# Infini-attention and grouped attention on one core: B's gate moved into the reciprocal sums, and the way from head sums to weighed heads cut into stages some turns apart

## The chip, the cores and the metric

The kernel runs on one core of a Trainium2 chip. The metric is device time in microseconds (us). The core's engines are TensorE (PE, with its weight loads shown as PEld), VectorE (DVE), ScalarE (ACT), GpSimd (POOL) and SyncE (SP), which issues nearly all DMA transfers.

## The reference

Two attentions over 2048 tokens, model width 576, 32 heads of width 18, in float32; their outputs stand side by side.

```
A:  q = x @ wq (32 heads); k = x @ wk, v = x @ wv (one head, shared)
    a = softmax(q k^T / sqrt(18)) v, heads side by side, @ wo
B:  q, k, v = x @ wq, x @ wk, x @ wv (32 heads each), in 4 segments of 512
    in each segment s, for each head, with g = sigmoid(beta[head]):
      a_dot = causal softmax(q k^T / sqrt(18)) v
      a_mem = (phi(q) M) / (phi(q) z + 1e-6)        # M = z = 0 in segment 0
      o     = g * a_mem + (1 - g) * a_dot
      M += phi(k)^T v;  z += sum of phi(k)          # phi(t) = t + 1 for t > 0, else exp(t)
    o, heads side by side, @ wo
```

## The kernel before, in words

The first stage (up to about 328 us) projects x for both attentions, stores q, k and v parts in DRAM, builds B's memory M and z, and stores for segments 1 to 3 the numerators already multiplied by g (`numB`, L353 and L354) and the denominators (`denB`). At its start ACT issues small loads, among them five of `b_beta` that spread each head's beta over the 18 rows of that head (L265 to L269). From these ACT and DVE make `gt`, which is g, and `omg`, which is 1 - g (L270 to L273).

The second stage works in blocks of four heads and 512 queries: 32 blocks of A (16 tiles of 128 keys) and 32 of B (three tiles, causal). B blocks come in pairs that a fixed list (L712) places behind A blocks. Two heads' scores for a tile of keys make an item, and three items make a turn (two at a block's end). In turn k the loop at L929 emits:

1. the scores of the turn's items on PE (L765 for A, L776 for B) and their exponentials on ACT (L785). One item of three is first copied out of PSUM by DVE (L782). Some exponentials of A are worked out on DVE in nine steps (L738 to L748), two steps in a turn. B's diagonal tiles are masked by POOL (L790);
2. one step of the output projection of a finished chunk, if one is waiting (`run_fill(1)`, L662: four matmuls; a chunk has 60 such steps);
3. the products with v of the items of turn k - 2 (L815). At a block's end DVE copies the sums out (L824) and SP stores them (L826). The first of a head's 19 rows is its sum of exponentials;
4. what is due by then (`due(k)`, L948): a list of pending steps, at most two in a turn.

A chunk is one attention's 512 queries. When its block 6 is done (heads 0 to 27, tiles 0 to 3) and again when its block 7 is done (heads 28 to 31, tile 4), `finish` (L868) puts the chunk's remaining steps on that list:

- `sums` one turn later: SP loads the sums of exponentials (`sm<-oA`, `sm<-oB`), and for B's segments 1 to 3 the denominators;
- `inverses` four or five turns after that: DVE's reciprocal (L618), then stores to DRAM (`rA`, `rB`, `rdB`);
- `load_heads`, tile by tile, when there is room (L890): the heads (`o`), the reciprocals spread over each head's 18 rows (`rb`), and for segments 1 to 3 the numerators (`nb`) and their reciprocals (`rb2`). It uses four buffers for rb and three each for nb and rb2;
- `weigh` six or eight turns later, one POOL operation at a time: for B o times omg (L647), o times rb (L644), nb times rb2 (L654) and their sum (L655); for A only o times rb;
- once all five tiles are weighed, the projection of the chunk joins the queue of fill steps.

PE, ACT and DVE run in exactly the order in which the loop emits (L918). POOL and SP do not: their order comes from the scheduler, and each runs its own queue in that order, as soon as the data are there. So the turn of a step fixes its place on PE, ACT and DVE, but on POOL a mask and a weighing step stand in whatever order the scheduler gave them. A transfer on SP also waits until the eighth one before it has landed.

Of the kernel before, what the change touches and what calls it, by code (L numbers as in the profile page):

```python
# [7 lines left out]
F32 = mybir.dt.float32  # L8
# [4 lines left out]
ALU = mybir.AluOpType  # L13
# [5 lines left out]
S, D, H, DH = 2048, 576, 32, 18  # L19
NSEG, L = 4, 512  # L20
C = 512
NCH = S // C
NKT = S // 128
HT = [7, 7, 7, 7, 4]
RT = [18 * h for h in HT]
H0 = [0, 7, 14, 21, 28]
# [7 lines left out]
VW = DH + 1  # L34
# [34 lines left out]
def attention_pair_kernel(ctx, tc, a_xT, a_w, a_wo, b_xT, b_w, b_wo, b_beta, ident_d, hmask_d, bmask_d, cmask_d, sel_d, zmask_d, selx_d, sely_d, out):  # L69
    nc = tc.nc  # L70
    ctx.enter_context(nc.allow_low_precision(reason="exact splits into parts"))

    cp = ctx.enter_context(tc.tile_pool(name="cp", bufs=1))
# [13 lines left out]
    oA = [dram(f"oA{c}", [H, 32, C], F32) for c in range(NCH)]  # L87
    oB = [dram(f"oB{c}", [H, 32, C], F32) for c in range(NSEG)]
    rA = [dram(f"rA{c}", [H, C], F32) for c in range(NCH)]
    rB = [dram(f"rB{c}", [H, C], F32) for c in range(NSEG)]  # L90
    rdB = [dram(f"rdB{c}", [H, C], F32) for c in range(NSEG)]
    numB = [dram(f"numB{c}", [D, C], F32) for c in range(NSEG)]
# [4 lines left out]
    kstA = cp.tile([128, S], F32R, name="kstA")  # L97
    VA = cp.tile([128, NKT * VW + 13], F32, name="VA")
    VAv = VA[:, : NKT * VW].rearrange("p (k v) -> p k v", v=VW)
    gt = cp.tile([128, 5], F32, name="gt")  # L100
    omg = cp.tile([128, 5], F32, name="omg")
    flag = cp.tile([1, 1], I32, name="flag")
    fm = cp.tile([128, 5], F32, name="fm")
    nc.gpsimd.memset(fm, 0.0)
# [40 lines left out]
    with ExitStack() as ph:  # L145
# [75 lines left out]
        for c in range(NCH):  # L221
            if c == 0:
                xh, xl, fillx = next_x(a_xT, 0)
                for k in range(5):
                    load_wk(wAh, wAl, a_w, 0, CA, k, True)
                    fillx(k)
                nc.sync.dma_start(ident, ident_d)
            else:
                xh, xl = nx[:2]
            nx = next_x(a_xT, c + 1) if c < NCH - 1 else next_x(b_xT, 0)  # L230
            for t in (4, 0, 1, 2, 3):
                M = 114 if t == 4 else 126
                pj = ps.tile([128, C], F32, name="pj", bufs=4)
                proj(pj[:M], wAh, wAl, xh, xl, 126 * t, M)
                R = RT[t]
                if t == 4:
                    nc.vector.tensor_reduce(km[:M, c : c + 1], pj[:M], axis=AX.X, op=ALU.max, apply_absolute_value=True)
                    vT = p1.tile([128, C], F32, name="vT", bufs=2)
                    nc.scalar.copy(vT[96:114], pj[96:114])
                    pv = ps.tile([128, 4, 128], F32, name="tr", bufs=1)  # L240
                    for i in range(4):
                        nc.tensor.transpose(pv[:, i, 0:DH], vT[96:114, 128 * i : 128 * i + 128], ident[96:114, 96:114])
                    nc.vector.tensor_copy(VAv[:, 4 * c : 4 * c + 4, 1:VW], pv[:, :, 0:DH])
                nc.scalar.activation(AQ[:R, t, c * C : c * C + C], pj[:R], AF.Abs)
                R2 = 90 if t == 4 else 126
                qp = split2(pt, pj[:R2], R2)
                store_parts(qp, 0, R, qA[c], H0[t], HT[t])
                nx[2](t)

                if c == 2:  # L250
                    load_wk(wBh, wBl, b_w, 504, 648, t, False)
                if c == 3:
                    load_wk(wBh, wBl, b_w, 2 * D, D, t, False)
                if t == 4:
                    nc.sync.dma_start(kA[:, :, c * C : c * C + C], qp[72:90].bitcast(F32))
            if c == 0:
                nc.scalar.dma_start(hmask[:126], hmask_d)
                nc.scalar.dma_start(bmask[:126], bmask_d)
                nc.scalar.dma_start(sel[:114], sel_d)
                nc.scalar.dma_start(zmask[:126], zmask_d)  # L260
                nc.scalar.dma_start(selx[:126], selx_d)
                nc.scalar.dma_start(sely, sely_d)
                nc.scalar.dma_start(ones_d.rearrange("j (a b) -> (j a) b", b=128), onest)
                nc.vector.memset(gt, 0.0)
                for t in range(5):  # L265
                    lo, nh = H0[t], HT[t]
                    nc.scalar.dma_start(
                        gt[: RT[t], t : t + 1], b_beta[lo : lo + nh][:, None].to_broadcast([nh, DH])[:, :, None]
                    )  # L269
                nc.scalar.activation(gt, gt, AF.Exp, scale=-1.0)  # L270
                nc.vector.tensor_scalar(gt, gt, 1.0, None, op0=ALU.add)
                nc.vector.reciprocal(gt, gt)
                nc.vector.tensor_scalar(omg, gt, -1.0, 1.0, op0=ALU.mult, op1=ALU.add)  # L273
# [339 lines left out]
        return sm, R, w, mem  # L613

    def inverses(ab, c, lo, hi, said):
        sm, R, w, mem = said
        n = 2 if mem else 1
        nc.vector.reciprocal(sm[:R, :n], sm[:R, :n])  # L618
        r_d = rA if ab == "A" else rB
        nc.sync.dma_start(r_d[c][lo:hi].rearrange("h (s t) -> h s t", t=w), sm[:R, 0])  # L620
        if mem:
            nc.sync.dma_start(rdB[c][lo:hi].rearrange("h (s t) -> h s t", t=w), sm[:R, 1])

    def load_heads(ab, c, t):
        o_d, r_d = (oA, rA) if ab == "A" else (oB, rB)
        if (ab, c) not in parts:
            parts[ab, c] = pa.tile([128, 5, C], F32, name="o", bufs=2)
        tiles = [parts[ab, c][:, t], pa.tile([128, C], F32, name="rb", bufs=4)]
        if ab == "B" and c > 0:
            tiles += [pa.tile([128, C], F32, name=n, bufs=3) for n in ("nb", "rb2")]  # L630
        lo, n, R = H0[t], HT[t], RT[t]
        nc.sync.dma_start(tiles[0][:R], o_d[c][lo : lo + n, 1:VW, :])
        nc.sync.dma_start(tiles[1][:R], r_d[c][lo : lo + n, None, :].to_broadcast([n, DH, C]))
        if ab == "B" and c > 0:
            nc.sync.dma_start(tiles[2][:R], numB[c][DH * lo : DH * lo + R])
            nc.sync.dma_start(tiles[3][:R], rdB[c][lo : lo + n, None, :].to_broadcast([n, DH, C]))
        return tiles

    def weigh(ab, c, t, tiles):

        R = RT[t]
        o, rb = (x[:R] for x in tiles[:2])
        v = nc.gpsimd
        own = lambda: v.tensor_tensor(o, o, rb, op=ALU.mult)  # L644
        if ab == "A":
            return [own]
        part = lambda: v.tensor_scalar(o, o, omg[:R, t : t + 1], None, op0=ALU.mult)  # L647
        if len(tiles) == 2:
            return [part, own]
        nb, rb2 = (x[:R] for x in tiles[2:])  # L650
        return [
            part,
            own,
            lambda: v.tensor_tensor(nb, nb, rb2, op=ALU.mult),  # L654
            lambda: v.tensor_tensor(o, o, nb, op=ALU.add),  # L655
        ]

    def out_part(ab, c, i, t, dst, c0, n, start, stop):

# [193 lines left out]
    def at(k, cost, ready, step):  # L853
        later.append((k, cost, ready, step))
        later.sort(key=lambda e: e[0])
# [12 lines left out]
    def finish(k, ab, c, hg):  # L868

        ts = range(4) if hg == 6 else range(4, 5)  # L870
        lo, hi = (0, 28) if hg == 6 else (28, 32)
        box = {}
        weighed.setdefault((ab, c), 0)
        last = (ab, c) == blocks[-1][:2]
        d1, d2 = (2, 3) if last else (4, 6) if (ab, c) == ("B", 0) else (5, 8)

        def begin(k):
            summing.add(hg)
            box[0] = sums(ab, c, lo, hi)
            at(k + d1, 0, lambda: True, inv)  # L880

        def inv(k):
            inverses(ab, c, lo, hi, box[0])
            summing.remove(hg)
            for t in ts:
                at(k, 0, room, lambda k, t=t: load(k, t))

        def room():

            return loaded[0] < (3 if ab == "B" and c > 0 else 4) and ((ab, c) in parts or len(parts) - filled[0] // FILL < 2)  # L890

        def load(k, t):
            loaded[0] += 1
            box[t, t] = load_heads(ab, c, t)
            at(k + d2, 1, lambda: True, lambda k, t=t: heads(k, t))

        def heads(k, t):
            if not isinstance(box[t, t][0], type(heads)):
                box[t, t] = weigh(ab, c, t, box[t, t])
            box[t, t].pop(0)()  # L900
            if box[t, t]:
                at(k, 1, lambda: True, lambda k: heads(k, t))
                return
            loaded[0] -= 1
            weighed[ab, c] += 1
            if weighed[ab, c] == 5 and not last:
                at(k + 1, 0, lambda: True, lambda k: fill.append(out_proj(ab, c)))

        at(k + (0 if last else 1), 0, lambda: hg not in summing, begin)

    def split(n, cut):

# [127 lines left out]
```

## Time and profile before

| | us |
|---|---|
| three timed runs | 1466.11, 1469.55, 1471.54 (median 1469.55) |
| the profiled execution | 1471.9 |
| its span, first to last instruction | 1470.2 |
| output projection, L662 (3680 matmul records) | from 486 us on, one step a turn |
| L790 masks on POOL | 94.2 (192) |
| L644 o times rb on POOL | 54.5 (40) |
| L647 o times omg on POOL | 32.6 (20) |
| L654, L655 on POOL | 21.4, 21.5 (15 each) |
| L745 on DVE, one of the exponential's steps | 142.4 (192), mean 0.741 |

Read the profile by turns: in the timeline of PE, from one group of score matmuls to the next is a turn, and its length is what counts. Each float32 matmul leaves two records. An idle engine matters only where the next turn starts late because of it.

### The profile page before, as it was taken

Reading aid. Unit: us, or ns where it says so; the run is one execution under the profiler, and the core shown is the slowest. Engines: PE = TensorE matmul, PEld = TensorE weight load, DVE = VectorE, ACT = ScalarE, POOL = GpSimd, SP = SyncE. Lnnn points to the kernel's source line nnn. Section 1 sums busy time; section 2 is a strip of 40 time slices with the busy share of each in tenths; the row PEclk is TensorE's granted clock in tenths of the full one; section 3 lists DMA queues with packets and bytes.
Section 4 is the critical chain, followed back from the end, with each engine's and each line's share of the span. In section 5 each row is a group of like instructions: output and inputs, shape, how many; then the busy total and the mean of one; then the engine's idle time right before and its main releaser. Section 6 shows DMA issues by size and latency. Waiting matters only on the chain.

```text
span 1470.2 us, 41131 instructions
## 1 busy us (share of the span) xinstructions
PE 1426.4 (97%) x17540; PEld 841.6 (57%) x17540; DVE 1080.7 (74%) x1529; ACT 1196.5 (81%) x1456; POOL 248.7 (17%) x311
## 2 busy tenths in 40 slices
PE   8979999999998999999999999999999999999998
PEld 5658878764454455545555545555555455555565
DVE  6574754647776688898778798787878988888861
ACT  3333334239998899999999999999999999999960
POOL 1031000001134212612110270131113400010001
PEclk9999999999999999999999999999999999999999
DMA  6775643446445154533222342233103220120022
GB/s 195 233 240 184 194 154 111 159 152 168 130 147 190 56 152 158 149 107 123 86 75 59 118 148 63 79 111 106 49 32 113 75 72 25 56 64 16 11 85 82
DMA packets 87989, 166.34 MB, mean 113 GB/s; under 512 B 12480, under 2 KB 21242, under 8 KB 87626
## 3 DMA queue, kind: packets, MB, share of 16 engines
q1 hardware_dynamic: 81510, 157.82, 34.3%
q10 hardware_dynamic: 6291, 5.85, 1.2%
q8 instruction: 138, 2.26, 0.6%
q14 instruction: 50, 0.40, 0.1%
HBM read 96.15 MB, written 67.49 MB: 111 GB/s over the span
## 4 chain that ended last, share of the span: by engine, by line
PE 64%; ACT 6%; DVE 3%; issue 3%; DMA 2%; SPq 1%; POOL 0%; ACTq 0%; DVEq 0%; POOLq 0%
PE O L815 29%; PE E L765 18%; PE F L662 11%; ACT P L785 5%; PE E L776 3%; DVE W L782 1%; PE E L662 1%; DMA rb<-rB 1%; PE O L662 1%; DMA rB<-sm 0%; DMA oB<-oe 0%; DMA sm<-oA 0%; DVE q L745 0%; DVE PD L748 0%; DVE n L747 0%
## 5 line engine op out<-in xcount | busy, mean ns | idle before, releaser
L785 ACT ACTIVATE P<-E 128x1024 f32<-128x1024 f32 (+1 forms) x800 | 806.2, 1120 | 12.3 <-PE E L776 4.4
L782 DVE COPY W<-E 128x1024 f32<-128x1024 f32 (+1 forms) x352 | 421.6, 1198 | 129.9 <-PE E L765 56.4
L815 PE MATMUL O<-P,VA 128*32 128x256 f32 x7680 | 510.4, 380 | 0.0
L785 ACT ACTIVATE P<-W 128x1024 f32<-128x1024 f32 (+1 forms) x352 | 411.7, 1170 | 6.9 <-DVE W L782 6.8
L815 PEld LDWEIGHTS O<-P,VA 128*32 128x32 f32 x7680 | 260.5, 110 | 139.8 <-issue 11.3
L765 PE MATMUL E<-stA,kstA 56*128 56x512 f32 x1920 | 327.3, 437 | 6.8 <-DVE W L782 4.0
L765 PEld LDWEIGHTS E<-stA,kstA 56*128 56x128 f32 x1920 | 155.3, 184 | 177.6 <-ACT P L785 79.1
L790 POOL TENSOR_SCALAR_AFFINE_SELECT P<-P 128x256 f32<-128x256 f32 (+1 forms) x192 | 94.2, 493 | 458.5 <-ACT P L785 425.5
L745 DVE SCALAR_TENSOR_TENSOR q<-q,PD 128x512 f32<-128x512 f32 x192 | 142.4, 741 | 3.1
L662 PE MATMUL F<-woB,o 126*32 126x192 f32 (+1 forms) x1920 | 127.5, 338 | 3.0 <-POOL o L644 3.0
L644 POOL TENSOR_TENSOR o<-o,rb 126x512 f32<-126x512 f32 (+1 forms) x40 | 54.5, 1363 | 323.6 <-DMA o<-oA 141.1
L815 PE MATMUL O<-P,vseg 128*32 128x256 f32 (+2 forms) x1536 | 83.9, 349 | 3.5 <-POOL P L790 3.5
L110 ACT CAST qp<-pj 126x512 fp32r<-126x512 f32 (+1 forms) x56 | 32.6, 584 | 62.1 <-DVE kmB L360 49.7
L662 PEld LDWEIGHTS F<-woB,o 126*32 126x32 f32 (+1 forms) x1920 | 38.4, 108 | 75.1 <-issue 64.4
L111 DVE TENSOR_TENSOR qp<-pj,qp 126x512 fp32r<-126x512 f32 (+1 forms) x56 | 38.3, 687 | 55.4 <-ACT qp L110 55.2
L662 PE MATMUL F<-woA,o 126*32 126x192 f32 (+1 forms) x1240 | 77.7, 338 | 1.1 <-DVE osb L687 1.1
L208 PE MATMUL pj<-xh,wBh 128*126 128x512 f32 x180 | 73.6, 413 | 3.1 <-DVE xh L180 3.1
L824 DVE COPY oe<-O 128x512 f32<-128x512 f32 x64 | 44.3, 692 | 41.0 <-PE O L815 40.3
L815 PE MATMUL O<-PD,VA 128*32 128x256 f32 x512 | 72.3, 382 | 0.0
L208 PE MATMUL pj<-xh,wBl 128*126 128x512 f32 x180 | 71.9, 400 | 0.0
L738 DVE TENSOR_SCALAR PD<-E 128x512 f32<-128x512 f32 x64 | 44.1, 689 | 31.7 <-PE E L765 24.5
L815 PEld LDWEIGHTS O<-P,vseg 128*32 128x32 f32 x1536 | 48.5, 111 | 30.3 <-POOL P L790 4.4
(136 smaller groups left out, 1580.4 us busy)
## 6 DMA issues: line engine op xcount, KB each, us to landing
stB<-kB SPq DMA_DIRECT2D x96, 144.0 KB
stB<-qB SPq DMA_DIRECT2D x32, 288.0 KB
stA<-qA SPq DMA_DIRECT2D x30, 288.0 KB
oA<-oe SPq DMA_DIRECT2D x32, 256.0 KB
oB<-oe SPq DMA_DIRECT2D x32, 256.0 KB
qA<-qp SPq DMA_DIRECT2D x16, 504.0 KB
kB<-qp SPq DMA_DIRECT2D x16, 504.0 KB
qB<-qp SPq DMA_DIRECT2D x16, 504.0 KB
```

The source lines that it names most:

```text
L208: nc.tensor.matmul(dst, w[:, c0 : c0 + M], x, start=i == 0, stop=i == len(ops) - 1)
L644: own = lambda: v.tensor_tensor(o, o, rb, op=ALU.mult)
L662: nc.tensor.matmul(dst[32 * j : 32 * j + 32], parts[ab, c][: RT[t], t, r0 : r0 + 32], wo[ab][: RT[t], t, c0 : c0 + n], start=start, stop=stop,
L738: v.tensor_scalar(p, e, LOG2, -116.0, op0=ALU.mult, op1=ALU.max)
L745: steps.append(lambda a=a: v.scalar_tensor_tensor(q, q, a, p, op0=ALU.add, op1=ALU.mult))
L765: nc.tensor.matmul(e[:, j], kstA[rows, 128 * kt : 128 * kt + 128], st[rows, h, :], start=True, stop=True)
L776: nc.tensor.matmul(e[:, j, c0 : c0 + 512 - 128 * k], st[rows, 4 + h, ks], st[rows, h, 128 * k :], start=True, stop=True)
L782: nc.vector.tensor_copy(src[:, :, :n], e[:, :, :n])
L785: nc.scalar.activation(p[:, :, :n], src[:, :, :n], AF.Exp, scale=SCALE)
L790: nc.gpsimd.affine_select(diag, diag, pattern=[[0, 2], [0, m], [1, 128]], base=0, channel_multiplier=-1, compare_op=ALU.is_ge, fill=0.0)
L815: nc.tensor.matmul(o[32 * j : 32 * j + 32, q0 : q0 + n], v, p[:, j % 2, p0 : p0 + n], start=m == hf == 0, stop=last and hf == 1,)
L824: nc.vector.tensor_copy(osb, o)
```

## The change

- Two more loads of `b_beta` at the start, columns 5 and 6 of gt and omg, hold each head's gate in the layout of the sums (4 rows a head for heads 0 to 27, 32 rows a head for heads 28 to 31).
- In `inverses` DVE multiplies B's reciprocal sums by omg, so that weighing has no product with omg.
- `load_heads` loads only the heads; a new `load_inverses` loads rb and, for B's segments 1 to 3, the numerators and their reciprocals, all in ten buffers named rb.
- `finish` places sums, heads, inverses and weighing by four distances d0 to d3. Heads wait for a place in the chunk's tile (`place`), the other loads for free buffers out of ten (`room`). The projection joins its queue two turns after the last weighing instead of one.

```diff
-    gt = cp.tile([128, 5], F32, name="gt")
-    omg = cp.tile([128, 5], F32, name="omg")
+    gt = cp.tile([128, 7], F32, name="gt")
+    omg = cp.tile([128, 7], F32, name="omg")
...
+                for t, lo, hi, n in ((5, 0, 28, 4), (6, 28, 32, 32)):
+                    nc.scalar.dma_start(
+                        gt[: n * (hi - lo), t : t + 1], b_beta[lo:hi][:, None].to_broadcast([hi - lo, n])[:, :, None]
+                    )
...
         nc.vector.reciprocal(sm[:R, :n], sm[:R, :n])
+        if ab == "B":
+            g = 5 if lo == 0 else 6
+            nc.vector.tensor_scalar(sm[:R, 0], sm[:R, 0], omg[:R, g : g + 1], None, op0=ALU.mult)
...
     def load_heads(ab, c, t):
-        tiles = [parts[ab, c][:, t], pa.tile([128, C], F32, name="rb", bufs=4)]
-        if ab == "B" and c > 0:
-            tiles += [pa.tile([128, C], F32, name=n, bufs=3) for n in ("nb", "rb2")]
...
+        nc.sync.dma_start(parts[ab, c][: RT[t], t], (oA if ab == "A" else oB)[c][H0[t] : H0[t] + HT[t], 1:VW, :])
+
+    def load_inverses(ab, c, t):
+        lo, n, R = H0[t], HT[t], RT[t]
+        tiles = [pa.tile([128, C], F32, name="rb", bufs=10)]
+        r_d = rA if ab == "A" else rB
+        nc.sync.dma_start(tiles[0][:R], r_d[c][lo : lo + n, None, :].to_broadcast([n, DH, C]))
         if ab == "B" and c > 0:
+            tiles += [pa.tile([128, C], F32, name="rb", bufs=10) for _ in range(2)]
+            nc.sync.dma_start(tiles[1][:R], numB[c][DH * lo : DH * lo + R])
+            nc.sync.dma_start(tiles[2][:R], rdB[c][lo : lo + n, None, :].to_broadcast([n, DH, C]))
         return tiles
...
-        part = lambda: v.tensor_scalar(o, o, omg[:R, t : t + 1], None, op0=ALU.mult)
...
+        steps = [lambda: v.tensor_tensor(o, o, rb, op=ALU.mult)]
...
-        box = {}
+        box, need = {}, 3 if ab == "B" and c > 0 else 1
...
-        d1, d2 = (2, 3) if last else (4, 6) if (ab, c) == ("B", 0) else (5, 8)
+        d0, d1, d2, d3 = (0, 2, 0, 3) if last else (2, 3, 3, 5) if (ab, c) == ("B", 0) else (2, 4, 3, 6)
...
-                at(k, 0, room, lambda k, t=t: load(k, t))
+                at(k, 0, place, lambda k, t=t: load(k, t))
+
+        def place():
+            return (ab, c) in parts or len(parts) - filled[0] // FILL < 2
+
+        def load(k, t):
+            load_heads(ab, c, t)
+            at(k + d2, 0, room, lambda k: weights(k, t))
 
         def room():
-            return loaded[0] < (3 if ab == "B" and c > 0 else 4) and ((ab, c) in parts or len(parts) - filled[0] // FILL < 2)
+            return loaded[0] + need <= 10
+
+        def weights(k, t):
+            loaded[0] += need
+            tiles = load_inverses(ab, c, t)
+            box[t, t] = weigh(ab, c, t, tiles)
+            at(k + d3, 1, lambda: True, lambda k: heads(k, t))
...
-                at(k + 1, 0, lambda: True, lambda k: fill.append(out_proj(ab, c)))
+                at(k + 2, 0, lambda: True, lambda k: fill.append(out_proj(ab, c)))
 
-        at(k + (0 if last else 1), 0, lambda: hg not in summing, begin)
+        at(k + d0, 0, lambda: hg not in summing, begin)
```

More of the change, by code (lines that the diff above doesn't have):

```diff
@@ L624, in load_heads @@
     def load_heads(ab, c, t):
-        o_d, r_d = (oA, rA) if ab == "A" else (oB, rB)
         if (ab, c) not in parts:
             parts[ab, c] = pa.tile([128, 5, C], F32, name="o", bufs=2)
-        tiles = [parts[ab, c][:, t], pa.tile([128, C], F32, name="rb", bufs=4)]
-        if ab == "B" and c > 0:
-            tiles += [pa.tile([128, C], F32, name=n, bufs=3) for n in ("nb", "rb2")]
-        lo, n, R = H0[t], HT[t], RT[t]
-        nc.sync.dma_start(tiles[0][:R], o_d[c][lo : lo + n, 1:VW, :])
@@ L633, in load_heads @@
-        nc.sync.dma_start(tiles[1][:R], r_d[c][lo : lo + n, None, :].to_broadcast([n, DH, C]))
-        if ab == "B" and c > 0:
-            nc.sync.dma_start(tiles[2][:R], numB[c][DH * lo : DH * lo + R])
-            nc.sync.dma_start(tiles[3][:R], rdB[c][lo : lo + n, None, :].to_broadcast([n, DH, C]))
+        nc.sync.dma_start(parts[ab, c][: RT[t], t], (oA if ab == "A" else oB)[c][H0[t] : H0[t] + HT[t], 1:VW, :])
[4 more added lines that the diff above has]
+        nc.sync.dma_start(tiles[0][:R], r_d[c][lo : lo + n, None, :].to_broadcast([n, DH, C]))
+        if ab == "B" and c > 0:
+            tiles += [pa.tile([128, C], F32, name="rb", bufs=10) for _ in range(2)]
+            nc.sync.dma_start(tiles[1][:R], numB[c][DH * lo : DH * lo + R])
+            nc.sync.dma_start(tiles[2][:R], rdB[c][lo : lo + n, None, :].to_broadcast([n, DH, C]))
@@ L637, in load_heads @@
         return tiles
     def weigh(ab, c, t, tiles):
-        R = RT[t]
-        o, rb = (x[:R] for x in tiles[:2])
+        o, (rb, *mem) = parts[ab, c][: RT[t], t], [x[: RT[t]] for x in tiles]
         v = nc.gpsimd
[L644 to L656, printed above, removed]
+        steps = [lambda: v.tensor_tensor(o, o, rb, op=ALU.mult)]
+        if mem:
+            nb, rb2 = mem
+            steps += [
+                lambda: v.tensor_tensor(nb, nb, rb2, op=ALU.mult),
+                lambda: v.tensor_tensor(o, o, nb, op=ALU.add),
+            ]
+        return steps
     def out_part(ab, c, i, t, dst, c0, n, start, stop):
@@ L885, in inv @@
             for t in ts:
-                at(k, 0, room, lambda k, t=t: load(k, t))
-        def room():
-            return loaded[0] < (3 if ab == "B" and c > 0 else 4) and ((ab, c) in parts or len(parts) - filled[0] // FILL < 2)
[L892 to L895, printed above, removed]
+                at(k, 0, place, lambda k, t=t: load(k, t))
[4 more added lines that the diff above has]
+            at(k + d2, 0, room, lambda k: weights(k, t))
+        def room():
+            return loaded[0] + need <= 10
[4 more added lines that the diff above has]
+            at(k + d3, 1, lambda: True, lambda k: heads(k, t))
         def heads(k, t):
-            if not isinstance(box[t, t][0], type(heads)):
-                box[t, t] = weigh(ab, c, t, box[t, t])
             box[t, t].pop(0)()
@@ L903, in heads @@
                 return
-            loaded[0] -= 1
+            loaded[0] -= need
             weighed[ab, c] += 1
             if weighed[ab, c] == 5 and not last:
-                at(k + 1, 0, lambda: True, lambda k: fill.append(out_proj(ab, c)))
-        at(k + (0 if last else 1), 0, lambda: hg not in summing, begin)
+                at(k + 2, 0, lambda: True, lambda k: fill.append(out_proj(ab, c)))
+        at(k + d0, 0, lambda: hg not in summing, begin)
     def split(n, cut):
```

## The prediction

> **What bounds the kernel now.** I read the busy shares first, then the waits, then the stretches in which waits gather.
>
> ```profile
> PE 1426.4 (97%) x17540; PEld 841.6 (57%) x17540; DVE 1080.7 (74%) x1529; ACT 1196.5 (81%) x1456; POOL 248.7 (17%) x311
> ```
>
> PE has work for 97% of the span, and the change removes no matmul. What can move is the 43.8 us without one (1470.2 - 1426.4) and turns that run long. From about 330 us on the timeline of PE is a row of turns, each led by a score group. With a piece of output projection an A turn takes 2.65 us, a B turn 2.2 to 2.8. Long turns lie in two kinds of places. The first is where PE waits for POOL. These are the rows for 430 to 510 us in the list of waits (us in total, times, longest):
>
> ```profile
> PE O L815 <- POOL P L790: 3.5, 2, 2.7
> PE F L662 <- POOL o L644: 3.0, 1, 3.0
> ```
>
> The causes stand in the timeline of POOL (start, length, line, operation, idle time before it):
>
> ```profile
> 449.52 4.65 POOL L647 TENSOR_SCALAR o<-o,omg 126x512 f32<-126x512 f32 x3 [20.98 <-DMA o<-oB]
> ...
> 455.69 1.29 POOL L644 TENSOR_TENSOR o<-o,rb 126x512 f32<-126x512 f32 x1 [0.27 <-DMA rb<-rB]
> 456.93 0.42 POOL L790 TENSOR_SCALAR_AFFINE_SELECT P<-P 128x256 f32<-128x256 f32 x1
> 457.52 1.28 POOL L644 TENSOR_TENSOR o<-o,rb 126x512 f32<-126x512 f32 x1 [0.17 <-DMA rb<-rB]
> 458.75 0.42 POOL L790 TENSOR_SCALAR_AFFINE_SELECT P<-P 128x256 f32<-128x256 f32 x1
> 459.31 1.56 POOL L647 TENSOR_SCALAR o<-o,omg 126x512 f32<-126x512 f32 x1
> 460.83 0.42 POOL L790 TENSOR_SCALAR_AFFINE_SELECT P<-P 128x256 f32<-128x256 f32 x1
> ```
>
> The causal masks (L790) of the next B block stand between weighing steps of B's first chunk, and these wait for transfers. PE's score groups start at 457.03, 463.89 and 467.33: 6.86 and 3.44 us for two turns of 2.33. That is 5.6 us lost. In the later turn PE's timeline shows the projection itself waiting:
>
> ```profile
> 496.19 1.15 PE L776 MATMUL E<-stB 56*128 56x512 f32 x6
> 500.31 0.87 PE L662 MATMUL F<-woB,o 72*32 72x192 f32 x8 [2.97 <-POOL o L644]
> ```
>
> The weighing of tile 4 ran only at 498.99, queued behind a mask. That turn took 7.47 us (to 503.66) against 2.77 for its kind, the next 2.53 against 2.23: 5.0 us.
>
> The second kind is DVE beside POOL. From the timeline of DVE, while POOL weighs without a pause:
>
> ```profile
> 866.07 1.20 DVE L742 SCALAR_TENSOR_TENSOR q<-PD 128x512 f32<-128x512 f32 x1
> 867.30 1.66 DVE L745 SCALAR_TENSOR_TENSOR q<-q,PD 128x512 f32<-128x512 f32 x1
> 868.89 1.21 DVE L782 COPY W<-E 128x1024 f32<-128x1024 f32 x1
> 870.02 2.37 DVE L745 SCALAR_TENSOR_TENSOR q<-q,PD 128x512 f32<-128x512 f32 x2
> ```
>
> Such a step takes 0.68 us elsewhere; the copy out of PSUM keeps its 1.21. The turns at 869.40 and 872.58 take 3.18 and 3.43 us. Taking each turn against the median of its kind, the stretches with weighing lose 1.3 (579 to 630), 2.2 (646 to 676), 3.3 (833 to 890), 0.5 (965 to 986) and 3.5 us (1119 to 1165): 10.8 in all.
>
> **The transfers.** The rows of the chain of waits give issue and time to landing:
>
> ```profile
> 433.48 5.76 DMA oB<-oe
> 442.17 6.14 DMA rB<-sm
> 451.77 9.15 DMA rb<-rB
> ```
>
> Landings in this stretch follow issue order, back to back: the head sums of tiles 0 to 3 at 433.09, vseg at 442.80, the last reciprocals' store at 461.12, although issued at 452.62. I treat SP's transfers as one line. An o load adds about 1.5 us to it, an rb load 1.5 to 1.8, vseg 3.6, the five pieces of wo 5.1.
>
> **The change, part by part.** The built instruction order shows where each step lands; on POOL and SP it is the scheduler's, and turn numbers do not bind it.
>
> *Start-up.* ACT issues two more gate loads; the five of before took 4.05 us of issue, 0.8 each, and the last landed 5.3 us after issue. One comes ahead of the fourth weight cast, one after. gt's exponential, which ran at 16.87, then waits for a load issued near 14.4 and landing at 18 to 19.7, and the fifth cast (18.21) is queued behind it. DVE's gate steps wait too, and behind them the x cast that PE awaited at 20.96. So PE starts that group 0 to 1.9 us later. Gaps of 1.7, 1.5 and 2.8 us at 50, 70 and 96 us may swallow some. I take +1.0.
>
> *First B chunk, sums and inverses.* The sums go out two turns after the block instead of one, now behind vseg; their reciprocal keeps its place on DVE (436.79). By the line of transfers they land near 441, so DVE waits some 4 us and the score copies (L782) behind it wait too. I price this at nothing, because the next wait covers it.
>
> *First B chunk, weighing.* In POOL's new order all five weighings stand ahead of the first mask of the next B block; before, tile 4's did not. Tile 4's rb goes after the second reciprocal store, which lands behind the four rb. The line from 431.76 holds the 27.8 us that before took from 433.09 to 460.92, plus the sums (0.25) and tile 4's o load (0.85): the fourth rb lands at 460.7, tile 4's some 2.4 later at 463. Behind it on SP stand the other loads of the next stB, wanted only at 496. With 1.3 us of weighing and three masks at 0.47, PE reaches its 463.89 point near 467. That is +3.0 against before. If the line loses its idle spots it is 0, with a transfer in front of tile 4 +4.5. Without this cover DVE's 4 us would show.
>
> The busy times by stretch bear on this (the third figure from the end is the granted clock): 0.82 over 453 to 468 us, in which PE waited for 2.71 us.
>
> ```profile
> 453.00:468.00 15.00, 11.54 (x130) 6.18 (x128) 5.59 (x6) 10.13 (x13) 13.33 (x18) 0.82 0.55 166
> ```
>
> The Trainium skill ("TensorE: Matmul & The Clock Gate", Part 1) puts the fall to half rate after an idle window of about 3.4 us. By it, a new wait of 3 us would leave the clock full and the term would be about 1.9 us smaller (the excess of the two turns after the stall), 1463 in place of 1465. The row shows a fall after a shorter wait, so I keep +3.0.
>
> *The wait at 500 goes.* Tile 4 is weighed by 465, and no weighing is left in front of the masks at 498: -5.0 (bounds -5.0 to -4.5). Late next is only ACT, at its usual pace.
>
> *POOL's 20 products with omg go:* 32.6 us of L647, of 130.0 us of weighing (54.5 + 32.6 + 21.5 + 21.4). If the 10.8 us lost shrink with POOL's time, a quarter goes, 2.7; a fall in density saves more, since a turn has slack before it runs long. For the three later B chunks the heads are loaded first, then three loads (some 4.6 us) bring 3.9 us of POOL work, where four loads brought 5.5. I take -3.0, between 0 and -6.5.
>
> *DVE's products with omg on the sums:* eight. The trace has 0.17 us (128x5) and 0.42 us (128x512) for such a step, so under 1.8 us in all; spread over turns with slack, between 0 and that, I take +0.3. The shorter way from the load of later sums to their reciprocal (four turns instead of five) I cost at nothing: at 565 us sums issued behind vseg would land near 572, DVE needs them near 574.
>
> *Projection steps.* They start at turn 57 instead of 60, pause three turns instead of two, and two fewer are left at the end, where PE is alone: 40 records take 1.63 us, so 16 take 0.65. -0.65. In the loop they lie under ACT, whose turns without a step are no shorter (2.7).
>
> *Shared buffers and prefetch.* Ten buffers as before in all. The numerators of chunks 2 and 3 load later, but they are not what lands last: 0. The last A chunk's loads end near 1441, PE needs them at 1461: 0.
>
> **Sum:** +1.0 + 3.0 - 5.0 - 3.0 + 0.3 - 0.65 = -4.35 us against the profiled execution (span 1470.2, 1471.9 with what lies around it), so 1467.5. That execution is above the median of 1469.55; on the median it is 1465.
>
> **Rivals.**
> - *Masks free early.* If the rb landed before about 455, both POOL waits would go: -5.4 in place of +3.0, 1457. For it: the chain's landings carry up to 9 us of queueing. Against it: the queue holds the same bytes. 0.17.
> - *Slower: tile 4's rb late.* Every mask now waits for it. In the trace of before it was issued at 469.26 and landed near 475, behind the loads of the next stB. If it falls behind them again, PE resumes near 479.5: +15.5 in place of +3.0, +8.2, 1478. From a landing at 467.5 on the change gains nothing; from 474 it loses over 0.5%. Against it: in the new order one stB load stands ahead of it, not sixteen. 0.13.
> - *Hidden anyway.* The weighing packs as tightly as before, so DVE loses the same 10.8 us, and the start-up costs its 1.9: -0.45, 1469. For it: before, four products spread thin (652 to 664 us) already cost 2.2 us. 0.18.
>
> **How the numbers follow.** The forecast holds 0.52, its own range 1460.5 to 1469. A difference under 0.5% (7.3 us) is about what a measurement of this kernel cannot tell from none. Faster by more: 0.17 and 0.06 of the forecast's lower end, 0.23. Slower by more: 0.13 and 0.02 for a start-up and a mask wait both at their ends, 0.15. Same: 0.62. From 1456 to 1471.5 the range takes in all but the slower rival and the lowest end of the first.
>
> **What would show it.** A DVE reciprocal that starts after 440; the first mask of the next B block behind a 72-row product near 463; no PE wait for POOL near 500; no L647 group; DVE's scalar_tensor_tensor nearer 0.68 on average (0.741 now); the score groups at 869 to 885 back under 3 us. The prediction is wrong where the first mask runs before 458 or after 467, or where DVE stands still at a later reciprocal.

## The result, and the profile after

The changed kernel takes 1476.09 us (median of 10 runs, 1472.27 to 1478.47) against 1471.05 of the kernel before (10 runs): a ratio of 1.0034, 95% interval 1.0017 to 1.0050. It is slower by 5 us, where 4.4 less was forecast, and outside the range of 1456 to 1471.5. The profiled execution took 1476.5 us with a span of 1474.8, 4.6 more than before's 1470.2. The busy times of its page:

```profile
PE 1431.1 (97%) x17540; PEld 850.8 (58%) x17540; DVE 1084.1 (74%) x1537; ACT 1195.9 (81%) x1456; POOL 219.1 (15%) x291
L750 DVE SCALAR_TENSOR_TENSOR q<-q,PD 128x512 f32<-128x512 f32 x192 | 141.9, 739 | 3.2
```

POOL has 20 instructions and 29.6 us less; DVE has 3.4 us more. L750 is before's L745: 0.739 us on average against 0.741. DVE was not relieved at all.

PE runs the same matmuls in the same order of turns, so the two rows of turns can be laid side by side. The lag of the changed kernel, turn by turn, says where the time went:

| turn that starts at (before) | lag, us | what lies between |
|---|---|---|
| 328.15 | 5.6 | first stage |
| 433.74 | 5.0 | |
| 491.44 | 9.4 | first B chunk: sums, masks |
| 546.66 | 4.6 | the wait at 500 |
| 1384.84 | 6.1 | weighing of the other chunks |
| last matmul | 4.8 | projection without scores |

So the start costs 5.0, the first B chunk 4.4, the wait at 500 gives back 4.8, the later weighing costs 1.5 and the end gives 1.3.

**The start.** PE's timeline of the kernel before and of the changed one (last column: idle time before, and what ended it):

```profile
20.96 0.46 PE L208 MATMUL pj<-xh,wAh 128*114 128x512 f32 x1 [1.04 <-DVE xh L184]
```

```profile
23.60 0.45 PE L209 MATMUL pj<-xh,wAh 128*114 128x512 f32 x1 [3.60 <-DVE xh L185]
...
24.70 0.63 PE L209 MATMUL pj<-xh,wAh 128*126 128x512 f32 x1
```

PE's second group, which starts with these rows, is 2.64 us late, and from 24.70 to 34 us its matmuls take 0.63 us, where before's took 0.39 up to 23 us and again from 29.22 on. The busy times by stretch (of the changed kernel, 20 to 25 and 25 to 36 us; the third figure from the end is the granted clock):

```profile
20.00:25.00 5.00, 1.40 (x5) 1.20 (x6) 3.44 (x8) 0.77 (x2) 0.00 (x0) 0.94 0.58 136
25.00:36.00 11.00, 9.31 (x27) 6.77 (x27) 8.88 (x13) 6.03 (x11) 4.05 (x2) 0.56 0.73 218
```

The lag grows to 4.2 us by the matmul that stood at 30.4, and is 3.9 at 300 us. The Trainium skill ("TensorE: Matmul & The Clock Gate", Part 1) lets the clock fall after an idle window of about 3.4 us: the gap of 3.60 agrees. But before's clock also fell, behind gaps of 0.84 and 1.39 with 0.42 us of small matmuls between them, 2.65 us in all, so that length is no safe bound here. Before's row for 25 to 30 us:

```profile
25.00:30.00 5.00, 4.30 (x12) 3.43 (x13) 4.97 (x6) 2.27 (x4) 3.30 (x2) 0.66 0.87 294
```

**The first B chunk.** The list of waits of PE, 434 to 515 us, and DVE's timeline:

```profile
PE O L820 <- POOL P L795: 3.9, 1, 3.9
PE E L770 <- DVE W L774: 3.4, 1, 3.4
```

```profile
446.55 0.95 DVE L624 RECIPROCAL sm<-sm 112x128 f32<-112x128 f32 x1 [4.65 <-DMA sm<-oB]
447.54 0.29 DVE L627 TENSOR_SCALAR sm<-sm,omg 112x128 f32<-112x128 f32 x1
```

The projection no longer waits for POOL near 500. In place of that wait, DVE stands still for 4.65 us at the reciprocal: the sums were issued behind vseg and landed at 446.53. The copy of scores behind it is late, and the turn of PE at 444.31 takes 8.22 us instead of 2.93. POOL's timeline shows the other wait, all five weighings ahead of the first mask:

```profile
461.41 2.66 POOL L654 TENSOR_TENSOR o<-o,rb 126x512 f32<-126x512 f32 x2 [27.85 <-DMA rb<-rB]
464.36 1.28 POOL L654 TENSOR_TENSOR o<-o,rb 126x512 f32<-126x512 f32 x1 [0.28 <-DMA rb<-rB]
466.32 1.28 POOL L654 TENSOR_TENSOR o<-o,rb 126x512 f32<-126x512 f32 x1 [0.69 <-DMA rb<-rB]
470.48 1.26 POOL L654 TENSOR_TENSOR o<-o,rb 72x512 f32<-72x512 f32 x1 [2.87 <-DMA rb<-rB]
471.69 3.87 POOL L795 TENSOR_SCALAR_AFFINE_SELECT P<-P 128x256 f32<-128x256 f32 x9
```

Tile 4's spread reciprocal landed at 470.35. The turn at 467.30 takes 7.94 us, the next two 1.89 and 2.30.

**DVE beside POOL.** The timelines of DVE and of POOL around 659 and 667 us:

```profile
658.78 1.68 DVE L747 SCALAR_TENSOR_TENSOR q<-PD 128x512 f32<-128x512 f32 x1
...
666.76 1.38 DVE L753 SCALAR_TENSOR_TENSOR PD<-q,n 128x512 f32<-128x512 f32 x1
668.18 1.40 DVE L745 TENSOR_SCALAR n<-PD 128x512 f32<-128x512 f32 x1
```

```profile
658.62 1.28 POOL L654 TENSOR_TENSOR o<-o,rb 126x512 f32<-126x512 f32 x1 [0.28 <-DMA rb<-rA]
666.32 2.98 POOL L654 TENSOR_TENSOR o<-o,rb 126x512 f32<-126x512 f32 x2 [6.41 <-DMA rb<-rA]
```

The step at 658.78 begins just behind a POOL product, which ends at 659.90, and ends itself 0.56 us later, where it takes 0.68 without POOL: it did nearly all of its work once POOL was done. A hit costs up to 1.1 us. The Trainium skill ("SBUF — State Buffer", Who interferes with whom) calls the pair of ports that DVE shares with GpSimd an exclusive lock, and says that a DVE instruction with two inputs from SBUF contends with a GpSimd instruction that reads SBUF; the rows agree. In before's trace the same look at the products with omg gives something else:

```profile
836.80 0.68 DVE L741 TENSOR_TENSOR PD<-PD,n 128x512 f32<-128x512 f32 x1
837.52 1.06 DVE L742 SCALAR_TENSOR_TENSOR q<-PD 128x512 f32<-128x512 f32 x1
```

```profile
835.76 3.15 POOL L647 TENSOR_SCALAR o<-o,omg 126x512 f32<-126x512 f32 x2 [0.64 <-DMA o<-oB]
```

The first step has two inputs and took its usual 0.68 beside such a product; the second lost 0.38. I add up, for every DVE step that reads SBUF and overlaps a POOL product, what it takes beyond the median of its kind without POOL, and put it down to the product with the larger overlap:

| products | before | after |
|---|---|---|
| o times rb (40) | 13.5 | 16.3 |
| o times omg (20) | 2.8 | gone |
| numerators times rb2 (15) | 3.8 | 3.7 |
| their sum (15) | 6.3 | 8.1 |
| all, us | 26.4 | 28.1 |

The products removed were the ones that held DVE least, 0.14 us each against 0.34 for the other 70, and those 70 happened to hit a little more often.

### The profile page after: what moved, and what is told of

The parts are those of the page before. It is cut to its first block, busy times and chain, and to the rows that moved or that the text cites. A ratio compares the mean times of both kernels' runs of the same rounds, so it can differ in the third digit from the quotient of the medians.

```text
span 1474.8 us, 41134 instructions
## 1 busy us (share of the span) xinstructions
PE 1431.1 (97%) x17540; PEld 850.8 (58%) x17540; DVE 1084.1 (74%) x1537; ACT 1195.9 (81%) x1456; POOL 219.1 (15%) x291
## 3 DMA queue, kind: packets, MB, share of 16 engines
q8 instruction: 138, 2.26, 0.6%
## 4 chain that ended last, share of the span: by engine, by line
PE 61%; ACT 6%; DVE 5%; issue 3%; DMA 2%; SPq 0%; POOL 0%; DVEq 0%; ACTq 0%; POOLq 0%
PE O L820 28%; PE E L770 17%; PE F L667 11%; ACT P L790 6%; PE E L781 3%; DVE W L787 2%; PE E L667 1%; PE O L667 1%; DMA sm<-oB 1%; DMA rB<-sm 1%; DVE q L750 0%; DVE sm L624 0%; DMA stA<-qA 0%; DVE PD L743 0%; DVE W L774 0%
## 5 line engine op out<-in xcount | busy, mean ns | idle before, releaser
L790 ACT ACTIVATE P<-W 128x1024 f32<-128x1024 f32 (+1 forms) x352 | 406.0, 1153 | 8.7 <-DVE W L787 8.4
L750 DVE SCALAR_TENSOR_TENSOR q<-q,PD 128x512 f32<-128x512 f32 x192 | 141.9, 739 | 3.2
```

What stands on the lines that cost most here:

```text
L750: steps.append(lambda a=a: v.scalar_tensor_tensor(q, q, a, p, op0=ALU.add, op1=ALU.mult))
L790: nc.scalar.activation(p[:, :, :n], src[:, :, :n], AF.Exp, scale=SCALE)
```

## The experiments

Beside each run stand its ratio to the kernel before, with its 95% interval (0.001 is 1.5 us), and lags of its turns behind before's, read as in the table above. A lag comes from one profiled execution. At 328 us it is 4.8 to 6.3 in the nine kernels with the two loads at the start, and -2.1 to -0.4 in the three without them, so it scatters by 1 to 2 us.

**1. The loads of beta moved away (gate_late).**

```diff
-                for t, lo, hi, n in ((5, 0, 28, 4), (6, 28, 32, 32)):
...
+            if k == 20:
+                for t, lo, hi, n in ((0, 0, 28, 4), (1, 28, 32, 32)):
+                    nc.scalar.dma_start(g2[...], b_beta[lo:hi]...)
+            if k == 30:
+                nc.scalar.activation(g2, g2, AF.Exp, scale=-1.0)
+            if k == 32:
+                nc.vector.tensor_scalar(g2, g2, 1.0, None, op0=ALU.add)
+                nc.vector.reciprocal(g2, g2)
+                nc.vector.tensor_scalar(omg2, g2, -1.0, 1.0, op0=ALU.mult, op1=ALU.add)
```

> The changed kernel, with the two extra loads of beta taken out of the start: they go to a tile of their own at turn 20 of the second stage, their exponential to turn 30, their three DVE steps to turn 32. Theory (the two loads delay the start, and the longer idle time of PE then halves its clock for a while): PE's second group starts at 21.0 instead of 23.6 us, the gap before it is near 1 instead of 3.6, and the first turn of the second stage starts at 328 to 330 instead of 333.7: 3 to 5 us off the time, 1471 to 1473. Rival (only the 2.6 us at PE's second group belong to the loads, the rest of the lag of 5.6 at 328 us is scatter): 2.6 off, the first turn at 331. The late steps themselves cost 0 to 1 us.

Measured: 1.0002 (0.9987 to 1.0017), 4.7 us off the changed kernel. PE's second group starts at 20.95 with a gap of 0.69, the lag at 328 us is -0.4 instead of 5.6. The theory holds: what the rival took for scatter behind the first 2.6 belongs in the main to the loads too. By 434 us the lag has grown by 1.2. The late steps stand there, but stages_behind (experiment 11), which has none, grows by 0.7 in the same stretch, so 1.2 is the most that they cost.

**2. The loads left, nothing made to wait for them (gate_apart).**

```diff
-    gt = cp.tile([128, 7], F32, name="gt")
+    gt = cp.tile([128, 5], F32, name="gt")
+    g2 = cp.tile([128, 2], F32, name="g2")
...
-                for t, lo, hi, n in ((5, 0, 28, 4), (6, 28, 32, 32)):
+                for t, lo, hi, n in ((0, 0, 28, 4), (1, 28, 32, 32)):
...
+            if k == 30:
+                nc.scalar.activation(g2, g2, AF.Exp, scale=-1.0)
```

> The changed kernel, with the two extra loads of beta left where they are but in a tile of their own, whose exponential and DVE steps come at turns 30 and 32 of the second stage: the first five columns wait for their own loads alone. Theory L (the loads of one element per row delay every landing behind them): the last pieces of A's weights still land near 20.2 and 20.8 instead of 17.5 and 18.1, PE's second group starts at 22.9 to 23.6, and the time is the changed kernel's within 1 us. Theory W (ACT and DVE wait in order for the late columns): the group starts at 21.0 to 21.5, and the time is that of the kernel with the loads moved away.

Measured: 1.0034 (1.0017 to 1.0052), lag at 328 us 5.9. PE's second group starts at 24.44, later even than theory L's 22.9 to 23.6. ACT's timeline:

```profile
18.07 0.21 ACT L278 ACTIVATE gt<-gt 128x5 f32<-128x5 f32 x1 [3.45 <-DMA gt<-b_beta]
21.69 0.71 ACT L200 CAST wAh<-wr 128x618 fp32r<-128x618 f32 x1 [3.41 <-DMA wr<-a_w]
```

The exponential ran early enough for PE to go on at 21, and the cast of the weights behind it still waited: the weights' last two pieces landed at 21.00 and 21.61, against 17.48 and 18.13 in before, though issued only 0.85 later. Theory L holds, theory W falls. The two loads carry 0.9 KB in pieces of 4 bytes, and the weights' pieces issued behind them land some 3 us later. That the size of the pieces is the reason is not shown: no run loads the same bytes in larger ones.

**3. Sums one turn earlier (sums_early).**

```diff
-        d0, d1, d2, d3 = (0, 2, 0, 3) if last else (2, 3, 3, 5) if (ab, c) == ("B", 0) else (2, 4, 3, 6)
+        d0, d1, d2, d3 = (0, 2, 0, 3) if last else (1, 4, 3, 5) if (ab, c) == ("B", 0) else (2, 4, 3, 6)
```

> The changed kernel, with the sums of B's first chunk loaded one turn earlier (d0 = 1, d1 = 4), ahead of vseg, the reciprocal in the same place. Both theories: the DVE wait of 4.7 us at the reciprocal and the turn of 8.2 us go. Theory line (SP's transfers land one after another, so the reciprocals' way back is not sooner): the fourth spread reciprocal still lands near 466 and tile 4's near 470, PE then waits longer for the masks, and the time stays within 1 us of the changed kernel's. Theory chain (the reciprocal was what held up the landings): all of it comes 4 to 5 us sooner and the time falls by 4 to 5, to 1471 to 1472.

Measured: 0.9995 (0.9982 to 1.0008), 5.7 us off. Both theories fail in a part. The time is that of theory chain. But the landings are those of theory line: the fourth spread reciprocal at 469.21 and tile 4's at 470.59, against 466.25 and 470.35. What they overlooked is POOL's order, which the edit changed too: the masks now stand between the weighings, and six of twelve run ahead of tile 4's. PE's longest wait for POOL falls from 3.9 to 2.4 us (434 to 515 us), and POOL's timeline ends with tile 4's weighing and the other six masks:

```profile
PE O L820 <- POOL P L795: 2.5, 2, 2.4
```

```profile
471.57 1.29 POOL L654 TENSOR_TENSOR o<-o,rb 72x512 f32<-72x512 f32 x1
472.80 2.75 POOL L795 TENSOR_SCALAR_AFFINE_SELECT P<-P 128x256 f32<-128x256 f32 x6
```

The lag goes from 6.2 at 434 to 5.5 at 491 us, where the changed kernel's goes from 5.0 to 9.4.

**4. Masks freed, with d2 (masks_free).**

```diff
-        d0, d1, d2, d3 = (0, 2, 0, 3) if last else (2, 3, 3, 5) if (ab, c) == ("B", 0) else (2, 4, 3, 6)
+        d0, d1, d2, d3 = (0, 2, 0, 3) if last else (2, 3, 8, 5) if (ab, c) == ("B", 0) else (2, 4, 3, 6)
```

> The changed kernel, with the spread reciprocals of B's first chunk loaded five turns later (d2 = 8), heads as before them: POOL's queue then has all masks of the next B block ahead of the weighing, and the rest of its order unchanged. Theory (the mask wait is POOL's place behind the weighing, and costs its own): the turn of 7.9 us near 467 falls to 2.3, the DVE wait of 4.7 at the reciprocal stays: 5 off, 1471. Rival (DVE's wait and the mask wait have one cause, so what one loses the other gains): no change beyond 1.

Measured: 1.0016 (1.0002 to 1.0030), 2.6 off. The list of waits of PE, 434 to 515 us:

```profile
PE E L770 <- DVE W L774: 3.5, 1, 3.5
PE E L770 <- ACT P L790: 1.1, 5, 0.3
```

The turn of 7.94 falls to 2.26, that of 8.22 stays: two waits one behind the other, each with its own price. The lag at 547 us is 0.2, 4.4 less than the changed kernel's, near the 5 expected; of that 1.7 is lost again by 1385, beside the weighing of the other chunks. So the time comes down by half of what the theory gave.

**5. Masks freed, with POOL in emitted order (weigh_behind).**

```diff
-    with tc.manual_schedule(engines={ENG.PE, ENG.Activation, ENG.DVE}):
+    with tc.manual_schedule(engines={ENG.PE, ENG.Activation, ENG.DVE, ENG.Pool}):
...
-        d0, d1, d2, d3 = (0, 2, 0, 3) if last else (2, 3, 3, 5) if (ab, c) == ("B", 0) else (2, 4, 3, 6)
+        d0, d1, d2, d3 = (0, 2, 0, 3) if last else (2, 3, 3, 13) if (ab, c) == ("B", 0) else (2, 4, 3, 6)
```

> The changed kernel, with POOL too in the order in which the loop emits, and the weighing of B's first chunk eight turns later (d3 = 13), so behind the masks of the next B block. Theory (these masks wait for nothing but POOL's place behind the weighing): PE's turn of 7.9 us near 467 falls to 2.3 to 2.8, the DVE wait of 4.7 at the reciprocal stays, two to three us go to a later projection and to turns that follow on; 3 to 5 us off, 1471 to 1473. Rival (the wait only moves: in the emitted order a weighing step stands ahead of masks elsewhere, or the projection waits for its heads): less than 1.5 off, with a new wait for POOL in the list.

Measured: 1.0040 (1.0027 to 1.0054). The turn near 470 falls to 2.25 as in experiment 4, the lag at 547 us is 2.2. Then it grows to 7.9 by 965 us, in turns beside weighing (3.85 and 4.30 us near 606 and 610). The time is the rival's, but its sign, a new wait for POOL, is not there: from 547 to 970 us PE waits for no POOL step, and 7.2 us for DVE's copies, against 1.5 in the changed kernel. DVE is held for 31.1 us against 28.1 in all. Why that order of POOL's hits DVE harder I did not take apart.

**6. The gate's move alone (fold_only).** The kernel before, with

```diff
-    gt = cp.tile([128, 5], F32, name="gt")
+    gt = cp.tile([128, 7], F32, name="gt")
...
+            nc.vector.tensor_scalar(sm[:R, 0], sm[:R, 0], omg[:R, g : g + 1], None, op0=ALU.mult)
...
-        part = lambda: v.tensor_scalar(o, o, omg[:R, t : t + 1], None, op0=ALU.mult)
```

> The kernel before, with only the gate's move: the two extra loads of beta, omg times the reciprocal sums, no product with omg at weighing; all stages as before. Theory hold (a DVE step waits for the end of a POOL product of two tiles, about 1 us a hit, and hardly for a product with a scalar): the turns beside weighing lose what they lost before (12.9 us over 580 to 1311) within 2; the start lies 5 to 6 later at 328 us; the stall of 5.6 at 457 to 467 shrinks by the POOL time of the five removed products between masks, 1 to 3: in all +2 to +4.5, a ratio of 1.0015 to 1.003. Rival (the loss goes with POOL's busy time): 3 less lost beside weighing, so -1 to +1.5, a ratio of 0.9995 to 1.001.

Measured: 1.0020 (1.0008 to 1.0031), and 26.8 us held on DVE against before's 26.4 with 20 products more. The lag is 5.5 at 434 us and -0.7 at 547: the stall at 457 shrinks by 1.4, as expected, and the wait at 500 goes without any of the stages. The time lies in the range of theory hold, but by luck: the 4.8 us won at 500 were not in its sum, and the stretch beside weighing loses 6.2 more than before (580 to 1311 us), where at most 2 were expected. Of these 6.2, 1.9 lie at 955 to 981 us: there the scheduler put A's weighing between masks, and these wait for its transfers.

```profile
961.00 1.28 POOL L651 TENSOR_TENSOR o<-o,rb 126x512 f32<-126x512 f32 x1 [2.29 <-DMA o<-oA]
962.24 0.60 POOL L795 TENSOR_SCALAR_AFFINE_SELECT P<-P 128x256 f32<-128x256 f32 x1
```

The other 4.3 I have not traced.

**7 and 8. Twenty products more, with a scalar or of two tiles (one_input, two_inputs).**

```diff
         steps = [lambda: v.tensor_tensor(o, o, rb, op=ALU.mult)]
+        if ab == "B":
+            steps.insert(0, lambda: v.tensor_scalar(o, o, omg[: RT[t], t : t + 1], None, op0=ALU.mult))
...
+        if ab == "B":
+            steps.insert(0, lambda: v.tensor_tensor(o, o, rb, op=ALU.mult))
```

> The changed kernel, with 20 more POOL products with a scalar at B's weighing (heads times omg once more, so B's first part is gated twice). Theory hold: DVE's excess beside POOL (24.6 us now) grows by 0.13 per product, 1 to 4 us, and the time by 0 to 2; at the masks near 467 up to 1.6 more. Rival (the loss goes with POOL's busy time, 32 us on 93): excess +8, time +4.

> The changed kernel, with 20 more POOL products of two tiles at B's weighing (heads times the spread reciprocal twice, so B's first part is divided twice). Theory hold: each product costs DVE 0.38 us as the 65 there do, excess +6 to +9 us, time +3 to +5. At the masks near 467 up to 1.3 more. If products of either kind cost DVE the same, it ends where the kernel with the 20 scalar products ends.

Measured: 1.0077 (1.0057 to 1.0097) and 1.0100 (1.0084 to 1.0117), some 6 and 10 us above the changed kernel. (The 24.6 us of the expectation count DVE's copies too; without them it is the table's 28.1.) On DVE the 20 scalar products hold 1.5 us, 3 of 26 steps beside them between 0.3 and 0.6 and one above; the 20 of two tiles hold 6.8, 7 of 14 steps, each by over 0.6. From 547 to 1385 us the lag changes by -0.4 and by +4.7, against the changed kernel's +1.5. So far that is theory hold. Its sums fail: over all products DVE is held for 24.4 and 29.6 us, where 1 to 4 and 6 to 9 above 28.1 were expected, because the other products hold less in both. Its times fail too, at most 3.6 and 6.3 us above the changed kernel; the 6 of one_input are nearer the rival's 4. The profiled execution of one_input took 1478.3 us, its six timed ones 1477.2 to 1484.9, and what the slower of them lost no trace shows. So time alone does not settle it.

**9. Thirty products of two tiles fewer (no_memory).**

```diff
-        if mem:
+        if False:
             nb, rb2 = mem
```

> The changed kernel, without the numerators' product and the sum at weighing (30 POOL products of two tiles less; the part from B's memory is left out of the output; its loads stay). Theory hold: 11.8 us of DVE's excess are put down to these 30; they go, and with them 5 to 7 us of the time: 1469 to 1471. Rival (DVE is held up by the weighing that is left, at its own phase, and turns have slack): less than 3 off.

Measured: 1.0077 (1.0057 to 1.0097): slower, which neither theory had. DVE is held for 7.7 us instead of 28.1, more than the 11.8 put down to these products, and outside one place the lag shrinks by 6.7 between 547 and 1385 us. At that place it grows by 7.9. POOL's timeline there:

```profile
959.03 1.29 POOL L654 TENSOR_TENSOR o<-o,rb 126x512 f32<-126x512 f32 x1 [2.37 <-PE E L781]
960.27 0.80 POOL L795 TENSOR_SCALAR_AFFINE_SELECT P<-P 128x256 f32<-128x256 f32 x2
961.14 1.27 POOL L654 TENSOR_TENSOR o<-o,rb 126x512 f32<-126x512 f32 x1
962.36 1.44 POOL L795 TENSOR_SCALAR_AFFINE_SELECT P<-P 128x256 f32<-128x256 f32 x2
```

As in experiment 6, A's weighing was put between the masks, and three turns of PE took 4.6, 6.7 and 4.5 us. What DVE no longer lost was real; POOL's order, which no one wrote, ate it.

**10 and 11. All three mended (late_early_behind), and the stages without the gate's move (stages_behind).** The first: the loads of experiment 1, issued by SP, and

```diff
-        d0, d1, d2, d3 = (0, 2, 0, 3) if last else (2, 3, 3, 5) if (ab, c) == ("B", 0) else (2, 4, 3, 6)
+        d0, d1, d2, d3 = (0, 2, 0, 3) if last else (1, 4, 8, 5) if (ab, c) == ("B", 0) else (2, 4, 3, 6)
```

The second: the same distances, five loads of beta, and omg back at weighing as in before.

> The changed kernel with all three mended: the extra loads of beta on SP at turn 20 of the second stage, the sums of B's first chunk one turn earlier, its spread reciprocals five turns later. If the three causes are separate and complete, 5 (start) + 5 (reciprocal) + 5 (masks) - 1 (late steps, projection three turns later) come off: 1461 to 1464, a ratio to the kernel before of 0.993 to 0.995; no wait of PE for POOL between 430 and 510, and first turn of the second stage at 328. If the reciprocal's and the masks' waits share one cause: 1466.

> The stages without the gate's move: no extra loads, the product with omg back on POOL, and B's first chunk with sums one turn earlier and spread reciprocals five turns later. Theory hold (products with a scalar hardly hold DVE): within 2 us of the kernel with all three mended, and without its late gate steps, 1460 to 1464. If POOL's busy time counts: 3 to 4 more than that kernel, 1465 to 1467.

Measured: 0.9960 (0.9945 to 0.9975), 1465.88 us, and 0.9956 (0.9939 to 0.9973), 1465.81 us. Both beat both kernels, by some 5.7 and 10 us. The first lost nothing between 434 and 547 us, where its lag goes from -1.2 to -11.3, so before's stall of 5.6 and wait of 5.0 are both gone. PE's longest waits from 430 to 515 us:

```profile
PE E L768 <- ACT P L788: 1.5, 6, 0.4
PE E L768 <- DVE W L785: 0.6, 1, 0.6
```

Its profiled execution (1462.5 us) is the fastest of its six; the median is 2 us above the expectation, and is the time given for a shared cause of the two waits. The lags speak against that: from 434 to 547 us sums_early gains 5.1 us on the changed kernel, masks_free 4.6, and this one 9.7, their sum. The second has the 20 scalar products back and is no slower, where 3 to 4 us were expected if POOL's busy time counts: from 547 to 1385 us its lag changes by +1.7, and that of the six variants with the gate's move and POOL's scheduled order (the changed kernel and experiments 1 to 4 and 10) by 0 to 3.2, 1.5 on average. So the gate's move is worth nothing here, within 2 us. What DVE is held for and the lag go together: the five kernels with 24 to 26 us held (gate_late, gate_apart, sums_early, one_input, stages_behind) change by -0.4 to +1.7 in that stretch, the four with 29 to 31 (masks_free, weigh_behind, two_inputs, late_early_behind) by 2.6 to 7.4. Only fold_only and no_memory, where masks wait near 960 us, stand outside this.

## Why the prediction was wrong

Step by step, forecast against the profiled execution:

- *Start-up, +1.0 (0 to +1.9): +5.0.* The step failed. I followed the two loads through ACT's and DVE's order, and priced no transfer behind them. Experiments 1 and 2 show that the order costs nothing and the landings cost the most of it: 2.6 us at PE's second group, 4.2 by 30 us behind a gap of 3.60 us and at a clock of 0.56, and 3.9 still at 300 us. The 1.1 more up to 434 us I have not traced; the three kernels without these loads at the start gain 0.6 to 1.2 of lag there too. A load landing at 18 to 19.7 us was right (19.61); what was behind it on the way was not counted.
- *DVE's wait at the reciprocal, 0, covered by the mask wait; masks, +3.0 (0 to +4.5): together +4.4.* DVE waited 4.65 us from 441.9 on, as worked out, and PE's row shows it as a stall of 5.3; PE passed its 463.89 point at 475.23, which is 470.2 with the lag of 5.0 taken off, 3 us later than the 467 reckoned: tile 4's spread reciprocal landed at 470.35 (465.4 in the same way) and not at 463. Two shorter turns behind gave 2.4 back, which was not reckoned, and so the sum is just within its bounds. The word "covered" holds only for POOL's order as built: experiments 3, 4 and 10 show two waits that can be taken away one by one, for some 4 to 5 us each.
- *The wait at 500, -5.0: -4.8.* Right, in place and in size; experiment 6 shows that the gate's move alone does it.
- *POOL's 20 products, -3.0 (0 to -6.5): +1.5.* The step failed: "if the 10.8 us lost shrink with POOL's time, a quarter goes". The loss doesn't go with POOL's time. A DVE step is held by a product of two tiles, which were all left; the products removed held 2.8 of 26.4 us, and experiment 11, which has them back, is no slower. The size of the +1.5 says little: six kernels with the same products change by 0 to 3.2. The rows were there: the steps of 1.20 and 1.66 us that I showed stand beside products of two tiles, and the steps beside L647 (836.80, 837.52) were not looked at by themselves.
- *DVE's products with omg, +0.3:* 0.29 and 0.23 us each, some 2.1 in all, in the same stretches; not to be told apart from the step above.
- *Fewer projection steps at the end, -0.65: -1.3.* Right in sign; the six kernels with the gate's move and POOL's scheduled order give -0.4 to -1.3, so the 0.7 more lies within what executions differ by.

The two failed terms make 4.0 and 4.5 of the 9 us between forecast and result. The rival "hidden anyway" had the second of them (DVE loses the same), and its price for the start, 1.9, was too small by 3. A rival with the transfers behind the two loads was missing. The time is near the 1478 of the rival "tile 4's rb late", but by luck: that load stood behind one load of the next stB, as forecast, and PE was 6.3 us later than before there (470.2 against 463.89), not the 15.5 that rival gave.

## What to carry to other kernels

A load that is spread into pieces of 4 bytes is priced by what stands behind it on its way, not by its own landing: 0.9 KB cost 4 to 5 us here, and moved to the second stage 1.2 at most. Work taken off an engine pays by the kind of instruction: look at the neighbour's steps beside each kind by itself before a loss is shared out by busy time. Where a scheduler orders one queue, every edit of the other queues reorders it, so read its new order for each edit, and compare two edits only where that order is the same.

## What was not expected of the hardware

- 20 POOL products with a scalar held DVE for 0.07 to 0.14 us each in three kernels (before, one_input, stages_behind), products of two tiles of the same size 0.34 to 0.40 (before, after, two_inputs). The Trainium skill ("SBUF — State Buffer", Who interferes with whom) says that a DVE instruction with two inputs from SBUF contends with a GpSimd instruction that reads SBUF, and does not set those with a scalar apart; the row of 836.80 and these sums do, and the measurement decides.
- Two loads of 0.4 and 0.5 KB, one element a row, delayed the landing of the 154.5 KB pieces behind them by 2.7 us (17.48 to 20.20) to 3.5 us (21.00, experiment 2).
